# Attention scores from the second batch on as three products of high and low parts, and feed-forward steps of twelve matmuls

## The chip, the core and the metric

One NeuronCore of a Trainium2 chip runs the whole program. The metric is the device time of one execution in microseconds; the kernel before takes 808.25 us (median of 3 runs, 807.92 to 809.6).

## What is computed

For batch 4, 8 heads, sequence 576 and head size 64, in float32:

```
q, k = rotate(q), rotate(k)
p = softmax(q @ k.T / sqrt(64));  x = p @ v            # x: 4 x 576 x 512
xk, xr = mu_k*x + (1-mu_k)*prev(x), mu_r*x + (1-mu_r)*prev(x)
x2 = sigmoid(xr @ w_r) * (relu(xk @ w_k)**2 @ w_v)     # 512 -> 1024 -> 512
h = relu(x2 @ w_in);  u, v = halves of h               # 512 -> 2 x 512
v = normalized rows of v;  v = w_spatial @ v + b
out = (u * v) @ w_out
```

## The kernel before, in words

PE is the TensorE matrix engine, DVE VectorE, ACT ScalarE, POOL GpSimd, SP the engine whose queue issues the DMAs. A matrix product comes in two forms. A product of float32 operands is exact; each is two instructions on PE, and each of these passes its columns twice. In the other form every operand is split into a high part (a copy rounded to fp32r, made by ACT) and a low part (the remainder, a subtraction on DVE), and three single-pass products are summed: high x high, low x high and high x low. The feed-forward and all later layers use the second form, the attention the first.

Heads are worked in pairs: one head of a pair lies in partitions 0 to 63, the other in 64 to 127 (`HEAD`), so that a [128, 576] tile holds q or k of two heads, transposed. There are 16 pairs of heads, `i = 4 * batch + p`. `prep(i)` (L213) loads a "raw" tile of k and one of q (each 128 x 2 x 576), multiplies it by cosines and sines (`times`, L229, DVE) and adds the two halves into a "rot" tile (`rope`, L234, DVE). Three raw and six rot buffers turn; a raw load waits until the sum of the tile three before is done, and a sum waits until the scores of the pair of heads three back are computed.

The attention runs in 72 units (`unit(m)`, L258), nine for two pairs of heads. A plain unit has 128 rows of q of both heads of one pair; every fifth of nine, the tail unit, has the last 64 rows of both pairs at once. A unit's `scores` (L267) are four products: two halves of 288 columns times the two heads. For a plain unit they read 64 partitions each, so the two heads use the upper and the lower row half of PE; the results go to two PSUM tiles of two banks. In a tail unit eight products use 64 x 64 quarters. Then come two maxima on DVE (L280), two exponentials on ACT (L285), transposes of the weights on PE (`turn`, L313 to L324, tile t), their copies by ACT and DVE (`take`, L334), the product with v on PE (`values`, L347, tile v, in column halves) and the final scaling (`gather`, L358, L360). The scores of the next unit wait for both exponentials of this one.

`feed(b, h)` (L399) is the feed-forward of one half (288 rows) of a batch: eight sums over four chunks (tile mk, L443, 12 matmuls each, in two steps of six), their relu, square and split, and four sums over eight chunks (tile mv, L483, 24 matmuls each, in four steps of six), copied by ACT to vs (L489) and stored (L492). The feed-forward of a batch is mixed with the attention of the next batch; that of the last batch comes after the attention. After all attention steps, `close` frees their memory and opens the buffers for the later layers' weights, which are loaded and split then.

No engine's order of work is written out by hand. Each step is added to a `Plan` with an engine, an estimated duration, what it depends on, a rank and, for some, a buffer to take; `Plan.order` (L59) plays the steps through, and takes for each engine, among the steps ready soonest (for engines other than PE within 0.3 us), the one of lowest rank. The instructions are issued in the order that comes out, and each engine keeps to it. Estimated durations only set the order.

The later layers (L602 on) are not touched.

Of the kernel before, what the change touches and what calls it, by code (L numbers as in the profile page):

```python
# [7 lines left out]
F32 = mybir.dt.float32  # L8
# [9 lines left out]
NP = H // 2  # L18
# [6 lines left out]
NFIRST = 2  # L25
WB, GB, WB2, GB2 = 3, 2, 3, 2
RAW, ROT, VB, PFB, PTB, XTS = 3, 6, 3, 3, 2, 6
KB, RLB, VSB = 4, 2, 4
WAIT = 0.3
# [3 lines left out]
def raw(ap):  # L33
    return ap.bitcast(F32)


class Step:


    def __init__(self, eng, us, fn, deps, rank, after, take, give, port):  # L40
        self.eng, self.us, self.fn, self.rank, self.after = eng, us, fn, rank, after
        self.take, self.give, self.slot = take, give, None
        self.port = port or eng == "POOL"
        self.deps = [d for d in deps if d is not None]
        self.end = self.begin = None


class Plan:
# [5 lines left out]
    def add(self, eng, us, fn, deps=(), rank=0.0, after=0.12, take=None, give=None, port=False):  # L54
        s = Step(eng, us, fn, deps, rank, after, take, give, port)
        self.steps.append(s)
        return s

    def order(self):  # L59
# [3 lines left out]
        left, port = len(self.steps), {"DVE": 0.0, "POOL": 0.0}  # L63
        while left:
            best = None
            for e, steps in todo.items():
                ready = []
                for s in steps:
                    if any(d.end is None for d in s.deps) or s.take and not room[s.take]:
                        continue  # L70
                    ready.append((max([free[e]] + [d.end + d.after for d in s.deps]
                                      + ([min(room[s.take])[0]] if s.take else [])
                                      + ([port["POOL" if e == "DVE" else "DVE"]] if s.port else [])), s))
                if ready:
                    soon = min(t for t, _ in ready) + (WAIT if e != "PE" else 0.0)
                    t, s = min((x for x in ready if x[0] <= soon), key=lambda x: (x[1].rank, x[0]))
# [12 lines left out]
            todo[s.eng].remove(s)  # L89
            left -= 1  # L90
# [8 lines left out]
def body(ctx: ExitStack, tc, qp, kp, vp, cs, mu_k, mu_r, w_k, w_v, w_r, w_in, w_sp, b_sp, w_out, out):  # L99
# [19 lines left out]
    cst = at.tile([128, 2, S], F32, name="cst")  # L119
    ident = const.tile([128, 128], F32, name="ident")  # L120
# [76 lines left out]
    def constants():  # L197
# [3 lines left out]
        nc.gpsimd.memset(ident, 0.0)  # L201
        nc.gpsimd.affine_select(out=ident, in_=ident, compare_op=ALU.not_equal, fill=1.0, base=0,
# [10 lines left out]
    def prep(i):  # L213
# [5 lines left out]
        for k in (1, 0):  # L219
# [22 lines left out]
            ropes["n", n] = add("DVE", 0.77, rope, [a] + last, need - 2.5, port=True)  # L242
# [15 lines left out]
    def unit(m):  # L258
# [8 lines left out]
        def scores():  # L267
            ps = st["s"] = [ps_s.tile([128, 2, 512], F32, tag="s", name=f"s{2 * m + j}") for j in range(2)]
            for u, (i, c) in enumerate(w):
# [7 lines left out]
            st["sm"] = at.tile([128, 4, 2], F32, tag="sm", bufs=4, name=f"sm{m}")  # L277
# [90 lines left out]
        scored[m] = s = add("PE", 2.2 if tail else 1.25, scores, need + [exps.get((m - 1, j)) for j in range(2)], m - 1.0)  # L368
# [12 lines left out]
        for n in range(3):  # L381
            turned[m, n] = add("PE", (0.55, 0.55, 0.3)[n], lambda slot, n=n: turn(n, slot), ready[n], m + 0.1 * n, take="t")
# [3 lines left out]
        if tail or part:  # L386
            v = add("PE", 1.6 if tail else 2.5, values, ev + [vloads[i] for i, _ in w], m + 0.9, take="m")
# [11 lines left out]
    def feed(b, h):  # L399
# [35 lines left out]
        for fc in range(NFC):  # L435
            def k_dot(n, slot=None, fc=fc):
# [3 lines left out]
                k = 6 * n  # L440
                for c in (2 * n, 2 * n + 1):
# [22 lines left out]
            z = add("PE", 0.84, lambda slot, k_dot=k_dot: k_dot(0, slot), done + wk_ready + [second.get("close")], rank(fc), take=room)  # L464
            p = add("PE", 0.84, lambda k_dot=k_dot: k_dot(1), [z], rank(fc) - 1)
# [9 lines left out]
        for dc in range(4):  # L475
            def v_dot(n, slot=None, dc=dc):
                if n == 0:
                    xs["v", dc] = bank(slot, f"mv{b}_{h}_{dc}")
                k = 6 * n
                for fc in (2 * n, 2 * n + 1):  # L480
# [13 lines left out]
            z = p = add("PE", 0.84, lambda slot, v_dot=v_dot: v_dot(0, slot), kk + wv_ready, rank(8 + 2 * dc), take=room)  # L494
            for n in range(1, 4):
                p = add("PE", 0.84, lambda n=n, v_dot=v_dot: v_dot(n), [p], rank(8 + 2 * dc) - 1)
# [33 lines left out]
    for m in range(NU):  # L530
# [303 lines left out]
```

## Time and profile before

| | |
|---|---|
| median of three runs | 808.25 us |
| the profiled execution | 808.49 us |
| its span (first to last instruction) | 806.5 us |
| PE, DVE, ACT, POOL busy | 766.6, 497.3, 443.6, 112.0 us |
| granted TensorE clock, mean | 0.991 of 2.4 GHz |

The span is shorter than the time of its execution by 2.0 us. In the profile, L275 is line 275 of the kernel. PE is the stream of matmuls, PEld that of its weight loads, which run beside it; an instruction's duration on PE holds its way through the pipeline, so successive instructions overlap and the distance between their starts tells what each takes of PE. A row's "x8" merges eight like instructions in succession: the first number is the start of the first, the second the time from there to the end of the last. "s" is the tile of the scores, "mk" and "mv" are the feed-forward's sums, "t" transposes, "v" the product with v. SPq is the DMA queue of SP.

### The profile page before, as it was taken

Reading aid. Unit: us, or ns where it says so; the run is one execution under the profiler, and the core shown is the slowest. Engines: PE = TensorE matmul, PEld = TensorE weight load, DVE = VectorE, ACT = ScalarE, POOL = GpSimd, SP = SyncE. Lnnn points to the kernel's source line nnn. Section 1 sums busy time; section 2 is a strip of 40 time slices with the busy share of each in tenths; the row PEclk is TensorE's granted clock in tenths of the full one; section 3 lists DMA queues with packets and bytes.
Section 4 is the critical chain, followed back from the end, with each engine's and each line's share of the span. In section 5 each row is a group of like instructions: output and inputs, shape, how many; then the busy total and the mean of one; then the engine's idle time right before and its main releaser. Section 6 shows DMA issues by size and latency. Waiting matters only on the chain.

```text
span 806.5 us, 14201 instructions
## 1 busy us (share of the span) xinstructions
PE 766.6 (95%) x5736; PEld 654.4 (81%) x5736; DVE 497.3 (62%) x885; ACT 443.6 (55%) x988; POOL 112.0 (14%) x128
## 2 busy tenths in 40 slices
PE   3898889999999999999999999988999999999998
PEld 2465557887887887887887899887999999998997
DVE  4988888966656746646635539889855242635211
ACT  3778786766756756756746755546533422523311
POOL 1332325000000000000000005564410000201000
PEclk9989999999999999999999999999999999999999
DMA  9445440431131131120110033375210202010101
GB/s 323 143 142 174 130 150 30 128 113 60 46 106 60 45 108 59 43 80 1 39 38 2 23 116 113 119 238 189 77 40 26 93 16 89 31 30 1 59 1 60
DMA packets 27555, 67.34 MB, mean 84 GB/s; under 512 B 4001, under 2 KB 8097, under 8 KB 27490
## 3 DMA queue, kind: packets, MB, share of 16 engines
q1 hardware_dynamic: 27490, 66.44, 25.2%
q8 instruction: 45, 0.74, 0.4%
q14 instruction: 20, 0.16, 0.1%
HBM read 52.26 MB, written 14.16 MB: 82 GB/s over the span
## 4 chain that ended last, share of the span: by engine, by line
PE 78%; DVE 8%; ACT 6%; issue 3%; DMA 3%; POOL 2%; SPq 0%; DVEq 0%; POOLq 0%; ACTq 0%
PE s L275 11%; PE v L347 11%; PE mv L483 10%; PE mk L443 9%; PE t L321 8%; PE sp L617 7%; PE o L617 6%; PE hv L681 5%; PE u L617 5%; PE r L617 4%; ACT pf L285 2%; PE t L313 1%; DMA I-120_121<-w_k 1%; DVE rl L453 1%; PE t L324 1%
## 5 line engine op out<-in xcount | busy, mean ns | idle before, releaser
L280 DVE TENSOR_REDUCE sm<-s 128x1 f32<-128x576 f32 x144 | 105.9, 751 | 37.0 <-PE s L275 36.2
L483 PE MATMUL mv<-kh,wv 128*128 128x288 f32 x512 | 117.0, 305 | 1.5 <-ACT kh L457 1.5
L443 PE MATMUL mk<-x,wk 128*128 128x288 f32 x768 | 117.4, 302 | 0.0
L285 ACT ACTIVATE pf<-s,sm 128x576 f32<-128x576 f32 x144 | 106.8, 744 | 15.8 <-DVE sm L280 14.3
L275 PE MATMUL s<-rot,rot 64*128 64x288 f32 (+1 forms) x640 | 103.6, 439 | 11.1 <-DVE rot L234 11.1
L334 ACT COPY pt<-t 128x512 f32<-128x512 f32 x144 | 83.2, 585 | 48.7 <-PE t L321 44.9
L443 PEld LDWEIGHTS mk<-x,wk 128*128 128x128 f32 x768 | 103.9, 188 | 6.1 <-issue 3.1
L321 PE MATMUL t<-ident,pf 128*128 128x128 f32 x512 | 81.7, 283 | 15.6 <-ACT pf L285 15.6
L483 PEld LDWEIGHTS mv<-kh,wv 128*128 128x128 f32 x512 | 85.8, 189 | 11.0 <-issue 9.2
L321 PEld LDWEIGHTS t<-ident,pf 128*128 128x128 f32 x512 | 57.8, 141 | 43.6 <-issue 19.0
L347 PE MATMUL v<-pt,vt 128*64 128x256 f32 (+1 forms) x960 | 92.2, 336 | 0.0
L275 PEld LDWEIGHTS s<-rot,rot 64*128 64x128 f32 (+1 forms) x640 | 57.5, 182 | 35.0 <-issue 11.1
L347 PEld LDWEIGHTS v<-pt,vt 128*64 128x64 f32 x960 | 56.2, 141 | 27.5 <-issue 7.2
L483 PE MATMUL mv<-kl,wv 128*128 128x288 f32 x256 | 75.7, 296 | 0.5 <-DVE kl L461 0.4
L617 PE MATMUL r<-xr,wr 128*128 128x288 f32 x384 | 53.4, 297 | 3.0 <-ACT vs L489 1.0
L617 PE MATMUL u<-x,wi 128*128 128x288 f32 x384 | 53.6, 302 | 2.5 <-ACT us L715 2.5
L617 PEld LDWEIGHTS u<-x,wi 128*128 128x128 f32 x384 | 53.0, 194 | 3.0 <-ACT us L715 2.8
L617 PEld LDWEIGHTS r<-xr,wr 128*128 128x128 f32 x384 | 51.6, 188 | 4.4 <-ACT rr L640 1.5
L229 DVE TENSOR_TENSOR raw<-raw,cst 128x1152 f32<-128x1152 f32 x32 | 44.5, 1389 | 16.9 <-DMA raw<-kp 9.2
L617 PE MATMUL sp<-ws,vn 128*128 128x288 f32 x384 | 53.9, 295 | 0.0
L617 PE MATMUL o<-g,wo 128*128 128x288 f32 x384 | 52.9, 296 | 0.5 <-ACT os L737 0.5
L617 PEld LDWEIGHTS sp<-ws,vn 128*128 128x128 f32 x384 | 52.4, 188 | 0.7
(332 smaller groups left out, 1091.5 us busy)
## 6 DMA issues: line engine op xcount, KB each, us to landing
raw<-kp SPq DMA_DIRECT2D x15, 576.0 KB, 4.9
raw<-qp SPq DMA_DIRECT2D x15, 576.0 KB, 3.8
vt<-vp SPq DMA_DIRECT2D x16, 320.0 KB, 3.7
xd<-xt SPq DMA_DIRECT2D x16, 288.5 KB, 3.1
vd<-vs SPq DMA_DIRECT2D x32, 144.0 KB, 1.8
v<-vd SPq DMA_DIRECT2D x16, 288.0 KB, 2.8
out<-os SPq DMA_DIRECT2D x16, 288.0 KB, 2.1
x<-xd SPq DMA_DIRECT2D x12, 288.5 KB, 3.0
```

What stands on the lines that cost most here:

```text
L229: nc.vector.tensor_tensor(t["raw", k], t["raw", k], cst, op=ALU.mult)
L275: nc.tensor.matmul(o, q[r, 128 * c:min(128 * c + 128, S)], k[r, h * HALF:(h + 1) * HALF], start=True, stop=True)
L280: nc.vector.tensor_reduce(st["sm"][:, 0, j:j + 1], st["s"][j][:, :, :HALF], axis=AX.XY, op=ALU.max, negate=True)
L285: nc.scalar.activation(st["p"][:, j, :].rearrange("p (a b) -> p a b", a=2), st["s"][j][:, :, :HALF], AF.Exp, bias=st["sm"][:, 0, j:j + 1], ...
L313: nc.tensor.transpose(pt.rearrange("p c (h q) -> p (c h) q", h=2)[:, 4 * u + c, :], p[HEAD[n], u, k:k + 128], ident[HEAD[n], HEAD[n]])
L321: nc.tensor.transpose(pt[:, c, :], p[:, n, k:k + 128], ident)
L334: nc.scalar.copy(o, x) if eng == "ACT" else nc.vector.tensor_copy(o, x)
L347: nc.tensor.matmul(o, v[:, 4 * j + c if c < 4 else 8 + j, :], a, start=c == 0, stop=c == 4)
L443: nc.tensor.matmul(ps[:, :HALF], wk[w][:, c, fc * 128:(fc + 1) * 128], a[:, c, :], start=k == 0, stop=k == 11)
L483: nc.tensor.matmul(xs["v", dc][:, :HALF], wv[w][:, fc, dc * 128:(dc + 1) * 128], a, start=k == 0, stop=k == 23)
L617: nc.tensor.matmul(ps[:, h, :HALF], w, a[:, h * HALF:(h + 1) * HALF], start=m == 0, stop=m == n - 1)
L681: nc.tensor.matmul(ps[:, :FS], x[a][:, d, c:c + 128], wi[w][:, d, FS:], start=k == 0, stop=k == 11)
```

## The change

From the second batch on (`EXACT = NP`, pairs of heads 4 to 15), q and k are split after the sum into a high part (ACT) and a low part (DVE), and the scores are three single-pass products in place of one exact product. In a plain unit these are still in row halves, twelve instructions in place of eight. In a tail unit, the 64 tail rows of both heads are also copied (high) and subtracted (low) into the two diagonal blocks of a 128 x 128 tile whose other blocks are zero (`ends`), so that the tail's products use the whole array: twelve instructions in place of sixteen. The sum is written over the raw tile, which so stays in use until the low part is there. Raw buffers go from 3 to 2; the six rot buffers become four for exact sums and high parts together, and four more for low parts; the buffers for vs go from 4 to 2. The scores of the pair of heads two back, not three back, now hold up the high copy. The feed-forward's steps have twelve matmuls in place of six, the same products in the same order. The planner's estimates for PE are new (with 0.1 us added when the kind of step changes), for existing steps too.

```diff
+EXACT = NP
-RAW, ROT, VB, PFB, PTB, XTS = 3, 6, 3, 3, 2, 6
-KB, RLB, VSB = 4, 2, 4
-WAIT = 0.3
+RAW, ROT, VB, PFB, PTB, XTS = 2, 4, 3, 3, 2, 6
+KB, RLB, VSB = 4, 2, 2
+WAIT, SWITCH, BONUS = 0.3, 0.1, 0.0
...
             s.begin, s.end = t, t + s.us
+            if s.eng == "PE" and s.kind != kind:
+                kind = s.kind
+                s.end += SWITCH
...
+    ends = [[at.tile([128, 128], F32R, tag=f"qe{i}{k}", name=f"qe{i}{k}") for k in range(2)] for i in range(2)]
...
             def rope(k=k):
-                x = t.pop(("raw", k))
-                y = t[k] = at.tile([128, S], F32, tag="rot", bufs=ROT, name=f"rot{i}_{k}")
+                x = t["raw", k]
+                y = t[k] = x[:, 0, :] if i >= EXACT else at.tile([128, S], F32, tag="rh", bufs=ROT, name=f"rot{i}_{k}")
                 nc.vector.tensor_tensor(y, x[:, 0, :], x[:, 1, :], op=ALU.add)
+            def high(k=k):
+                t["hi", k] = at.tile([128, S], F32R, tag="rh", bufs=ROT, name=f"rh{i}_{k}")
+                nc.scalar.copy(t["hi", k], t[k])
+                if k == 0:
+                    for j in range(2):
+                        nc.scalar.copy(ends[i % 2][0][HEAD[j], 64 * j:64 * j + 64], t[k][HEAD[j], 512:])
+            def low(k=k):
+                t["lo", k] = at.tile([128, S], F32R, tag="rl", bufs=ROT, name=f"rl{i}_{k}")
+                nc.vector.tensor_tensor(t["lo", k], t[k], raw(t["hi", k]), op=ALU.subtract)
+                if k == 0:
+                    for j in range(2):
+                        r, z = HEAD[j], slice(64 * j, 64 * j + 64)
+                        nc.vector.tensor_tensor(ends[i % 2][1][r, z], t[k][r, 512:], raw(ends[i % 2][0][r, z]),
+                                                op=ALU.subtract)
...
-            ropes["n", n] = add("DVE", 0.77, rope, [a] + last, need - 2.5, port=True)
+            if i < EXACT:
+                ropes["n", n] = add("DVE", 0.77, rope, [a] + last, need - 2.5, port=True)
+            else:
+                a = add("DVE", 0.77, rope, [a], need - 2.5, port=True)
+                a = add("ACT", 0.67 if k else 1.1, high, [a] + last, need - 2.5)
+                ropes["n", n] = add("DVE", 0.76 if k else 1.2, low, [a], need - 2.5, port=True)
...
+            if w[0][0] >= EXACT:
+                for u, (i, c) in enumerate(w):
+                    t = qk[i]
+                    for n, (a, b) in enumerate((("hi", "hi"), ("hi", "lo"), ("lo", "hi"))):
+                        for h in range(2):
+                            x, f = slice(h * HALF, h * HALF + HALF), dict(start=n == 0, stop=n == 2)
+                            if tail:
+                                nc.tensor.matmul(ps[u][:, h, :HALF], ends[i % 2][a == "lo"], t[b, 1][:, x], **f)
+                            else:
+                                for j, r in enumerate(HEAD):
+                                    nc.tensor.matmul(ps[j][:, h, :HALF], t[a, 0][r, 128 * c:128 * c + 128], t[b, 1][r, x], **f)
+                return
...
-        scored[m] = s = add("PE", 2.2 if tail else 1.25, scores, need + [exps.get((m - 1, j)) for j in range(2)], m - 1.0)
+        scored[m] = s = add("PE", (2.0 if tail else 1.07) if w[0][0] < EXACT else 1.58 if tail else 0.8, scores, need + [exps.get((m - 1, j)) for j in range(2)], m - 1.0, kind="s")
...
-            z = add("PE", 0.84, lambda slot, k_dot=k_dot: k_dot(0, slot), done + wk_ready + [second.get("close")], rank(fc), take=room)
-            p = add("PE", 0.84, lambda k_dot=k_dot: k_dot(1), [z], rank(fc) - 1)
+            z = p = add("PE", 1.58, lambda slot, k_dot=k_dot: k_dot(0, slot), done + wk_ready + [second.get("close")], rank(fc), take=room)
...
-            for n in range(1, 4):
-                p = add("PE", 0.84, lambda n=n, v_dot=v_dot: v_dot(n), [p], rank(8 + 2 * dc) - 1)
+            for n in range(1, 2):
+                p = add("PE", 1.58, lambda n=n, v_dot=v_dot: v_dot(n), [p], rank(8 + 2 * dc) - 1)
...
-            if i not in ropes and i >= ROT // 2 and max(which_last(i - 3)) <= m:
+            if i not in ropes and i >= ROT // 2 and max(which_last(i - ROT // 2)) <= m:
```

## Rows read from the trace of the kernel before

**Rows 1.** The page: busy us (share of the span) by engine; the chain by engine.

```profile
PE 766.6 (95%) x5736; PEld 654.4 (81%) x5736; DVE 497.3 (62%) x885; ACT 443.6 (55%) x988; POOL 112.0 (14%) x128
...
PE 78%; DVE 8%; ACT 6%; issue 3%; DMA 3%; POOL 2%; SPq 0%; DVEq 0%; POOLq 0%; ACTq 0%
```

**Rows 2.** Windows: length, busy PE, PEld, DVE, ACT, POOL (count), clock, DMA, GB/s.

```profile
60.00:117.00 57.00, 49.00 (x366) 31.90 (x364) 49.94 (x97) 45.65 (x111) 15.42 (x14) 0.97 0.47 151
117.00:180.00 63.00, 62.60 (x510) 51.11 (x509) 53.46 (x91) 41.85 (x104) 12.28 (x15) 1.00 0.30 95
180.00:240.00 60.00, 59.94 (x486) 48.36 (x486) 37.55 (x72) 37.92 (x95) 0.20 (x2) 1.00 0.22 71
```

**Rows 3.** PE's waits, 0 to 117 us, then 117 to 470 (total, times, longest).

```profile
PE t L321 <- ACT pf L285: 15.2, 11, 2.3
PE s L275 <- DVE rot L234: 11.1, 1, 11.1
...
PE t L321 <- ACT pf L285: 0.4, 1, 0.4
```

**Rows 4.** Timelines of two short windows, PE: pairs of one score block.

```profile
408.11 0.65 PE L275 MATMUL s<-rot,rot 64*128 64x288 f32 x3
...
408.35 0.64 PE L275 MATMUL s<-rot,rot 64*128 64x288 f32 x3
```

**Rows 5.** Timeline, PE: the score block of a plain unit and its neighbours.

```profile
414.84 0.29 PE L483 MATMUL mv<-kh,wv 128*128 128x288 f32 x1
415.06 1.24 PE L275 MATMUL s<-rot,rot 64*128 64x288 f32 x8
416.24 0.40 PE L483 MATMUL mv<-kh,wv 128*128 128x288 f32 x1
416.47 0.29 PE L483 MATMUL mv<-kl,wv 128*128 128x288 f32 x1
```

**Rows 6.** The same timeline: a long feed-forward run and a tail unit.

```profile
428.17 3.43 PE L443 MATMUL mk<-x,wk 128*128 128x288 f32 x24
431.44 0.60 PE L321 MATMUL t<-ident,pf 128*128 128x128 f32 x4
431.96 2.16 PE L275 MATMUL s<-rot,rot 64*64 64x288 f32 x16
434.05 0.66 PE L321 MATMUL t<-ident,pf 128*128 128x128 f32 x4
```

**Rows 7.** Timelines of short windows, weight loads (PEld).

```profile
400.77 0.19 PEld L483 LDWEIGHTS mv<-kh,wv 128*128 128x128 f32 x1
400.88 0.19 PEld L483 LDWEIGHTS mv<-kl,wv 128*128 128x128 f32 x1
...
407.76 0.30 PEld L275 LDWEIGHTS s<-rot,rot 64*128 64x128 f32 x4 [0.17 <-issue]
```

**Rows 8.** Groups by form, DVE, then ACT: busy us, mean ns | idle before, releaser.

```profile
L229 DVE TENSOR_TENSOR raw<-raw,cst 128x1152 f32<-128x1152 f32 x32 | 44.5, 1389 | 16.9 <-DMA raw<-kp 9.2 <-DMA raw<-qp 7.6
...
L461 DVE TENSOR_TENSOR kl<-rl,kh 128x576 fp32r<-128x576 f32 x32 | 24.3, 760 | 5.4 <-ACT kh L457 5.1
...
L304 DVE COPY pe<-pf 128x64 f32<-128x64 f32 x32 | 5.9, 227 | 0.6
...
L457 ACT CAST kh<-rl 128x576 fp32r<-128x576 f32 x32 | 21.5, 673 | 8.5 <-DVE rl L453 7.9
```

**Rows 9.** The chain that ended last, in order of time: an earlier tail unit.

```profile
129.32 2.09 PE s L275 x16
```

**Rows 10.** The page: groups of DVE and ACT in the chain of a unit.

```profile
L280 DVE TENSOR_REDUCE sm<-s 128x1 f32<-128x576 f32 x144 | 105.9, 751 | 37.0 <-PE s L275 36.2
```

**Rows 11.** The page: DMA issues, KB each, us to landing.

```profile
raw<-kp SPq DMA_DIRECT2D x15, 576.0 KB, 4.9
...
vd<-vs SPq DMA_DIRECT2D x32, 144.0 KB, 1.8
```

**Rows 12.** The DMA queue's own waits (total, times, longest).

```profile
SPq L224 <- DVE rot L234: 110.2, 19, 19.9
```

More of the change, by code (lines that the diff above doesn't have):

```diff
@@ L37, with __init__ @@
 class Step:
-    def __init__(self, eng, us, fn, deps, rank, after, take, give, port):
+    def __init__(self, eng, us, fn, deps, rank, after, take, give, port, kind):
         self.eng, self.us, self.fn, self.rank, self.after = eng, us, fn, rank, after
         self.take, self.give, self.slot = take, give, None
-        self.port = port or eng == "POOL"
+        self.port, self.kind = port or eng == "POOL", kind
         self.deps = [d for d in deps if d is not None]
@@ L52, in __init__, with add @@
         self.steps, self.room = [], room
-    def add(self, eng, us, fn, deps=(), rank=0.0, after=0.12, take=None, give=None, port=False):
-        s = Step(eng, us, fn, deps, rank, after, take, give, port)
+    def add(self, eng, us, fn, deps=(), rank=0.0, after=0.12, take=None, give=None, port=False, kind=None):
+        s = Step(eng, us, fn, deps, rank, after, take, give, port, kind)
         self.steps.append(s)
@@ L62, in order @@
         todo = {e: [s for s in self.steps if s.eng == e] for e in free}
-        left, port = len(self.steps), {"DVE": 0.0, "POOL": 0.0}
+        left, port, kind = len(self.steps), {"DVE": 0.0, "POOL": 0.0}, None
         while left:
@@ L75, in order @@
                     soon = min(t for t, _ in ready) + (WAIT if e != "PE" else 0.0)
-                    t, s = min((x for x in ready if x[0] <= soon), key=lambda x: (x[1].rank, x[0]))
+                    t, s = min((x for x in ready if x[0] <= soon), key=lambda x: (x[1].rank - (BONUS if e == "PE" and x[1].kind == kind else 0.0), x[0]))
                     if best is None or t < best[0]:
@@ L201, in constants @@
         nc.gpsimd.memset(ident, 0.0)
+        for x in ends[0] + ends[1]:
+            nc.gpsimd.memset(raw(x), 0.0)
         nc.gpsimd.affine_select(out=ident, in_=ident, compare_op=ALU.not_equal, fill=1.0, base=0,
@@ L268, in scores @@
             ps = st["s"] = [ps_s.tile([128, 2, 512], F32, tag="s", name=f"s{2 * m + j}") for j in range(2)]
+            st["sm"] = at.tile([128, 4, 2], F32, tag="sm", bufs=4, name=f"sm{m}")
+            if w[0][0] >= EXACT:
[10 more added lines that the diff above has]
+                return
             for u, (i, c) in enumerate(w):
@@ L276, in scores @@
                                          start=True, stop=True)
-            st["sm"] = at.tile([128, 4, 2], F32, tag="sm", bufs=4, name=f"sm{m}")
         def top(j):
@@ L381, in unit @@
         for n in range(3):
-            turned[m, n] = add("PE", (0.55, 0.55, 0.3)[n], lambda slot, n=n: turn(n, slot), ready[n], m + 0.1 * n, take="t")
+            turned[m, n] = add("PE", (0.44, 0.44, 0.22)[n], lambda slot, n=n: turn(n, slot), ready[n], m + 0.1 * n, take="t", kind="t")
             eng = ("ACT", "ACT", "DVE")[n]
@@ L386, in unit @@
         if tail or part:
-            v = add("PE", 1.6 if tail else 2.5, values, ev + [vloads[i] for i, _ in w], m + 0.9, take="m")
+            v = add("PE", 1.1 if tail else 2.2, values, ev + [vloads[i] for i, _ in w], m + 0.9, take="m", kind="v")
             for u, (i, c) in enumerate(w):
@@ L439, in k_dot @@
                 ps, (xh, xl) = xs["k", fc], xs["x"]
-                k = 6 * n
-                for c in (2 * n, 2 * n + 1):
+                k = 0
+                for c in range(NP):
                     for a, w in ((xh, 0), (xl, 0), (xh, 1)):
@@ L478, in v_dot @@
                     xs["v", dc] = bank(slot, f"mv{b}_{h}_{dc}")
-                k = 6 * n
-                for fc in (2 * n, 2 * n + 1):
+                k = 12 * n
+                for fc in range(4 * n, 4 * n + 4):
                     kh, kl = (t[:, fc % 2, :] for t in xs["kk", fc // 2])
```

2 lines of the change are left out of this document (1 added, 1 removed).

## The prediction

> **What bounds the kernel now.** I read the page's shares first: PE is busy for 95% of the span and PE lines make 78% of the chain that ended last [rows 1]. A share is an average, so the windows come next. The reader is to see three stages there. Until about 115 us the first batch's attention runs alone: PE is busy for 49.0 of 57 us and DVE for 49.9. From 117 to 470 us the attention of the other three batches is mixed with the feed-forward of the batch before: PE is busy for 59.9 of every 60 us, DVE for 53.5 of 63 at first and some 37.5 of 60 later, ACT for about 38. The granted clock is 0.97 to 1.00, the upper of its two levels, 2.4 GHz [rows 2]. The last 336 us belong to code that the change does not touch, save for the feed-forward of the last batch. A busy PE may be a PE that waits inside its pipeline, so the third view is PE's waits: in the first batch 11.1 us for the first scores and 15.2 for exponentials, and from 117 to 470 no more than 0.4 us in all [rows 3]. In those 353 us nothing but PE's own work sets the pace, so whatever PE is spared there moves the end of the attention, if DVE and ACT can still follow. What is after hangs on that end: `close` waits for all attention steps, and the later layers' weights are loaded behind it.
>
> **Scores of a plain unit (48 units, L275).** Today's eight instructions (four products, each passed through PE as two) come as pairs, one per row half; successive pairs start 0.24 us apart (408.11, 408.35) [rows 4]. Four pairs are 0.97 us. The block takes more than that: from the feed-forward product before it (414.84) it starts 0.22 us later where such products follow each other in 0.13; from its start to the next product are 1.18; and that product takes 0.23 where 0.13 is usual [rows 5]. In all 0.09 + 1.18 + 0.10 = 1.37 us, so 0.40 are for getting into the row halves and out. I take those 0.40 over unchanged: the new block is in row halves too.
>
> The new block has six pairs of single-pass products of 288 columns. The trace has no such pair. Its nearest row is the feed-forward product of the same type and width on the full array, 0.13 us apart (0.132 each over the 24 from 428.17 to 431.44, less 0.10 for the first) [rows 6]. That the two halves run beside each other is what the pairs show: an exact instruction streams its columns twice, which by the transposes (128 columns in (431.96 - 431.44 - 0.09)/4 = 0.108) is 0.24 for 288 columns, and a pair takes just that [rows 4, 6]. So a pair is 0.132, six are 0.79, and a plain unit gives back 0.97 - 0.79 = 0.18: **48 x 0.18 = 8.6 us**. Bounds: 0.12 a pair (half of 0.243) gives 11.7; products one after another, 12 x 0.132 = 1.58, cost 29 (rival below).
>
> Weights are loaded twelve times, not eight. The four loads of the first two pairs are done in 0.30 us where one takes 0.19, so the second pair is 0.11 behind the first; single loads of the full array also start 0.11 apart (400.77, 400.88) [rows 7]. Two half loads take the time of one full load, 0.11, and hide below 0.132. The Trainium skill (TensorE: Matmul & The Clock Gate, LDWEIGHTS) says that loading takes time by columns and no less with fewer rows, which speaks against this change; if the twelve loads queued one by one, its 107 ns would make about 1.28 us of a block, and the sum would turn into a loss of some 11 us. The rows differ for two loads of different halves, and I go by the rows.
>
> **Scores of a tail unit (6 units).** Today: 0.09 to enter and 2.09 from 431.96 to 434.05, 2.18 in all [rows 6]. New: twelve full-array products, 12 x 0.132 = 1.58, which stand beside transposes and feed-forward on the full array and so have no row halves or quarters to get into. What the step still costs is at most the 0.10 seen behind a score block [rows 5], and I set it off against the like cost behind today's block, which I left out. The zero blocks are written once at the start. **6 x 0.60 = 3.6 us** (bounds 3 and 4.2).
>
> **Feed-forward in steps of twelve.** The products are the same. From the last product of a run to the transpose behind it there is no gap beyond 0.13 (the 24 products of [rows 6]), and the 0.40 of a score block is paid once a unit whatever its neighbours, so merging saves little: **0.5 us**, at most one entry of 0.05, half of 0.10, for each of 54 units, 2.7. What it may cost is attention that becomes ready just after a step of 1.58 us has begun; that is PE time used, not lost, while the chain s, two maxima, one exponential (1.2 + 1.5 + 0.9, some 3.6 us, the maximum 0.75 [rows 10]) is far below the 6.7 us of a unit ((431.96 - 129.32)/45, tail to tail [rows 6, 9]). I take nothing, and make the other case a rival.
>
> **High and low parts of q and k (12 pairs of heads).** DVE gets per pair two subtractions of 0.76 and two small ones of 0.23; ACT two copies of 0.67 and two small ones, which I put at half of that at most [rows 8]. That is 2.0 us each a pair, 24 in all. Cover: from 180 us DVE has 37.6 + 8 = 45.5 of 57.6 us per batch and ACT the same, 79%, below the 85% at which DVE stood from 117 to 180 without PE waiting [rows 2]. In 117 to 180, three pairs add 6 to DVE's 53.5, and one pair of heads fewer is prepared ahead (bufs 6 to 4), which takes 2 x 1.39 for the products with cosines and sines and 2 x 0.76 for the sums away, 4.3 [rows 8]: about 55 of 60, 91%. The first batch stood at 88% and PE waited there. I put **2 us** of new waits there, between 0 and 9 (15.2 us of waits over 18 units [rows 3], for the eleven units of that window).
>
> **First batch.** Its scores stay exact. Pair 4 and perhaps 5 are split there: 2 us of DVE each, on an engine at 88%. Raw buffers go from 3 to 2, so the second pair of heads' first load now waits for the first sum, which is done just before the first scores at 11.1 [rows 3]; it lands 4.9 us later [rows 11], and its scores are those of the fifth unit. Loads behind it on SP's queue are placed by the planner. **1.5 us** slower, between -1 and 4.
>
> **Queues.** Raw loads already hold SP's queue for 110 us in 19 waits [rows 12], with stores of vs and xt and loads of v behind them. From the second batch a raw buffer stays until the low part exists: 4.9 to land, 1.4 for the product, 0.8 for the sum, 0.7 and 0.8 for the two parts, and the wait for the scores two pairs back. A pair of heads has about 30 us, so both buffers turn in time. A vs store lands in 1.8 us [rows 11] and the same buffer is wanted two outputs, 6.3 us, later: two instead of four cost nothing; if late, ACT waits, and then the bank.
>
> **Sum.** The profiled execution took 808.5 us (806.5 of span and 2.0 around it), as good as the median of 808.25. -8.6 - 3.6 - 0.5 + 2 + 1.5 = -9.2: **799.3 us**.
>
> **Rivals.**
> A. *As summed*: 791 to 804 (0.12 a pair and no new waits; or waits of 7 us).
> B. *DVE or ACT takes PE's place* until about 180 us: 4 us in the first batch and 9 after, against 13 gained: 808.5, no change. For it: 91% and 88%. Against: DVE waited for others there for some 10 of 63 us, and steps are ordered by the planner, which counts the new work. 804 to 813.
> C. *The halves do not run side by side for single-pass products*, in each of the 48 plain score blocks. It decides above (0.97 + 0.08)/6 = 0.175 us a pair (0.08 is a 48th of the 3.6 of the tails). Products in line, 0.264 a pair, give 48 x 0.61 = 29, and 808.5 + 29 - 4.1 + 3.5 = 837. Loads in line, 2 x 0.11 a pair, give 48 x 0.35 = 17 and 825. Against: both loads and products of two halves start together in the exact form. Slower.
> D. *Long feed-forward steps make attention late*: half of the added 0.79 us on each of 54 units, 21 us, if the chain of a unit set the pace: about 820. Against: 3.6 of 6.7 us. A part of it, 812, is likelier.
> E. *Not doing what it says*: the switch at EXACT = NP is plain in the code; no chance of its own.
>
> **Numbers.** A 0.70, B 0.15 (0.05 faster, 0.06 same, 0.04 slower), C 0.07, D 0.08 (0.01 same). About 0.2%, 1.6 us, can be told from no change. Faster 0.75, same 0.07, slower 0.18. The range 791 to 812 leaves out C, most of D and the edges of A and B, some 0.18; A's own range is 791 to 804.
>
> **What would show it.** Score pairs 0.12 to 0.14 us apart and blocks of about 1.0 us to the next product; tails of 1.6; units 6.5 us apart from 117 us on; PE waits below 3 us in that stretch; `close` 8 to 12 us earlier, and the stages after it as long as before. PE waits on `low` or on exponentials would speak for B or D, score blocks above 1.3 us for C. I am wrong if PE is no longer without waits there.

## The result, and the profile after

The changed kernel takes 795.91 us (median of four executions, 793.3 to 797.58) against 808.09. The ratio on record is 0.9836, with a 95% interval of 0.9811 to 0.986 (the two medians alone would give 0.985); the percentages below go by such ratios. The forecast was 799.3 us in a range of 791 to 812, with rival A the likeliest. The profiled execution took 797.47 us, with a span of 795.4.

The page of the kernel after, the lines that answer to [rows 1]:

```profile
PE 752.4 (95%) x5904; PEld 664.2 (84%) x5904; DVE 509.7 (64%) x933; ACT 461.2 (58%) x1036; POOL 112.9 (14%) x132
...
PE 83%; DVE 5%; ACT 4%; DMA 3%; issue 3%; POOL 1%; SPq 0%; ACTq 0%; DVEq 0%; POOLq 0%
```

PE has 168 instructions more and 14.2 us less to do; DVE has 12.4 us more and ACT 17.6. The windows of the kernel after, with the columns of [rows 2], and the stretch in the middle by itself:

```profile
60.00:117.00 57.00, 50.81 (x408) 34.21 (x404) 50.96 (x104) 48.71 (x121) 15.09 (x14) 1.00 0.44 137
117.00:180.00 63.00, 60.16 (x501) 52.10 (x499) 52.50 (x94) 43.61 (x107) 13.91 (x15) 0.92 0.28 89
180.00:240.00 60.00, 60.00 (x540) 52.33 (x540) 43.54 (x85) 43.01 (x108) 0.20 (x2) 1.00 0.24 72
142.40:152.70 10.30, 9.24 (x42) 7.32 (x44) 8.28 (x12) 6.03 (x16) 3.42 (x2) 0.50 0.01 2
```

From 180 us to the end of the attention PE is still never idle, and DVE and ACT stand at 73% and 72% there: they have room for the new parts. Between 117 and 180 the granted clock is now 0.92. PE's waits in the kernel after, first from 0 to 117 us and then from 117 to 470, which answer to [rows 3]:

```profile
PE t L361 <- ACT pf L325: 11.9, 10, 1.8
PE s L316 <- DVE rot L241: 10.6, 1, 10.6
...
PE t L361 <- ACT pf L325: 2.2, 1, 2.2
PE t L364 <- ACT rb L336: 0.7, 1, 0.7
```

Two new waits, 2.9 us in all, stand where 0.4 were. Now the score blocks, against [rows 4 to 6] (timeline of PE after, a plain unit at 165 us, then a tail unit and what follows it):

```profile
164.49 0.60 PE L361 MATMUL t<-ident,pf 128*128 128x128 f32 x4
165.02 0.53 PE L308 MATMUL s<-rh,rh 64*128 64x288 f32 x4
165.38 0.43 PE L308 MATMUL s<-rl,rh 64*128 64x288 f32 x4
165.65 0.42 PE L308 MATMUL s<-rh,rl 64*128 64x288 f32 x4
166.00 0.66 PE L361 MATMUL t<-ident,pf 128*128 128x128 f32 x4
...
304.79 0.42 PE L305 MATMUL s<-rh,qe 128*128 128x288 f32 x2
...
306.39 0.60 PE L361 MATMUL t<-ident,pf 128*128 128x128 f32 x4
...
306.93 0.27 PE L364 MATMUL t<-ident,rb 128*128 128x128 f32 x1
306.96 1.83 PE L483 MATMUL mk<-x,wk 128*128 128x288 f32 x12
308.72 2.38 PE L387 MATMUL v<-pt,vt 128*64 128x256 f32 x20
311.03 0.54 PE L308 MATMUL s<-rh,rh 64*128 64x288 f32 x4
...
312.04 1.86 PE L483 MATMUL mk<-x,wk 128*128 128x288 f32 x12
313.82 1.02 PE L353 MATMUL t<-ident,pf 64*128 64x64 f32 x16
```

and the weight loads (PEld) at the start of the same plain block:

```profile
165.02 0.30 PEld L308 LDWEIGHTS s<-rh,rh 64*128 64x128 f32 x4 [0.17 <-issue]
```

Four products of the two halves take 0.27 us (165.38 to 165.65): two pairs, 0.135 each. The plain block takes 0.98 from its start to the next transposes, where the exact one took 1.18, and the tail 1.60 (304.79 to 306.39) where it took 2.09. One more thing is to be seen: twelve feed-forward products take 1.76 us (306.96 to 308.72) and 1.78 (312.04 to 313.82), 0.18 to 0.20 more than 12 x 0.132. It is tempting to call that the price of a visit to the feed-forward, but most of it is there without the visit too. The transpose ahead of the first visit takes 0.03 (306.93 to 306.96) where 0.108 is usual, and four transposes followed by scores at once take 0.53 (164.49 to 165.02), 0.10 more than 4 x 0.108. So from the last transpose to the product with v (306.93 to 308.72) 1.79 pass, 0.21 more than the twelve products; with no visit the last of the four transposes takes 0.53 - 3 x 0.108 = 0.21 as well (the three times in units 36 to 63 that a product with v follows transposes at once, it is 0.20). A visit costs something where it stands right behind a score block or a product with v: from 311.03 to 313.82 less 1.58 are 1.21, where a block followed by transposes of 128 rows takes 0.98.

To see where the time went, the span is cut at the starts of units 18, 27 and 71. Worked out from the first score product of each unit on PE's timeline, in us:

```
                    to unit 18   18 to 27   27 to 71   from 71   span
before                 104.4       60.6      294.0      347.5    806.5
after                  101.0       64.0      281.6      348.8    795.4
```

The 44 units from 27 on give 12.4 us, 0.28 each; the nine before them cost 3.4; the stages after the attention are about as long as before (+1.3). The 3.4 of the first batch can't be put down to the change alone: in the kernel before, the granted clock stood at its lower level for 10.2 us there, after not at all (1.00 in its window against 0.97 in [rows 2]).

### The profile page after: what moved, and what is told of

Read it like the earlier page. It is cut to its first block, busy times and chain, and to the rows that moved or that the text cites. A ratio compares the mean times of both kernels' runs of the same rounds, so it can differ in the third digit from the quotient of the medians.

```text
span 795.4 us, 14650 instructions
## 1 busy us (share of the span) xinstructions
PE 752.4 (95%) x5904; PEld 664.2 (84%) x5904; DVE 509.7 (64%) x933; ACT 461.2 (58%) x1036; POOL 112.9 (14%) x132
## 4 chain that ended last, share of the span: by engine, by line
PE 83%; DVE 5%; ACT 4%; DMA 3%; issue 3%; POOL 1%; SPq 0%; ACTq 0%; DVEq 0%; POOLq 0%
PE mk L483 11%; PE v L387 11%; PE mv L522 10%; PE t L361 9%; PE sp L656 7%; PE o L656 6%; PE s L308 6%; PE u L656 6%; PE r L656 5%; PE hv L720 5%; PE s L316 3%; ACT pf L325 1%; PE s L305 1%; ACT pt L374 1%; PE t L364 1%
## 5 line engine op out<-in xcount | busy, mean ns | idle before, releaser
L483 PE MATMUL mk<-x,wk 128*128 128x288 f32 x768 | 114.3, 301 | 0.0
L522 PE MATMUL mv<-kh,wv 128*128 128x288 f32 x512 | 112.1, 303 | 0.0
L361 PE MATMUL t<-ident,pf 128*128 128x128 f32 x512 | 83.4, 286 | 14.1 <-ACT pf L325 14.1
L361 PEld LDWEIGHTS t<-ident,pf 128*128 128x128 f32 x512 | 57.6, 142 | 37.4 <-issue 15.4
L656 PE MATMUL r<-xr,wr 128*128 128x288 f32 x384 | 56.6, 308 | 5.3 <-ACT xr L616 2.7
L656 PEld LDWEIGHTS r<-xr,wr 128*128 128x128 f32 x384 | 54.7, 199 | 6.8 <-ACT xr L616 3.2
L656 PEld LDWEIGHTS o<-g,wo 128*128 128x128 f32 x384 | 51.7, 188 | 1.4 <-ACT os L776 1.2
L522 PEld LDWEIGHTS mv<-kl,wv 128*128 128x128 f32 x256 | 48.8, 191 | 0.6 <-DVE kl L501 0.6
```

The lines of the kernel that those rows point to most:

```text
L361: nc.tensor.transpose(pt[:, c, :], p[:, n, k:k + 128], ident)
L483: nc.tensor.matmul(ps[:, :HALF], wk[w][:, c, fc * 128:(fc + 1) * 128], a[:, c, :], start=k == 0, stop=k == 11)
L522: nc.tensor.matmul(xs["v", dc][:, :HALF], wv[w][:, fc, dc * 128:(dc + 1) * 128], a, start=k == 0, stop=k == 23)
L656: nc.tensor.matmul(ps[:, h, :HALF], w, a[:, h * HALF:(h + 1) * HALF], start=m == 0, stop=m == n - 1)
```

## The experiments

All twelve start from the kernel after. Theory "scores": the gain is PE time of the score blocks, as summed. Its rivals: the feed-forward's steps give it, or the planner's new estimates do.

**Each of the two parts alone, and neither.** Feed-forward steps of six again, the products and their order as before the change:

```diff
-                k = 0
-                for c in range(NP):
+                k = 6 * n
+                for c in (2 * n, 2 * n + 1):
...
-            z = p = add("PE", 1.58, lambda slot, k_dot=k_dot: k_dot(0, slot), done + wk_ready + [second.get("close")], rank(fc), take=room)
+            z = add("PE", 0.79, lambda slot, k_dot=k_dot: k_dot(0, slot), done + wk_ready + [second.get("close")], rank(fc), take=room)
+            p = add("PE", 0.79, lambda k_dot=k_dot: k_dot(1), [z], rank(fc) - 1)
...
-                for fc in range(4 * n, 4 * n + 4):
+                for fc in (2 * n, 2 * n + 1):
```

> The changed kernel with the feed-forward again in steps of six matmuls (estimate 0.79 us each), all else as changed. Theory: the gain is the shorter scores, and the steps' length matters little: 796 to 798 us, at most 2 more than the changed kernel; the score block costs the same 1.06 us of PE a unit, and t and mk cost some 0.1 us a unit more because single steps come more often between s, v and t. Rival (the merged steps are a main part of the gain, as a unit went from 6.68 to 6.40 us where the scores alone explain 0.22): 800 us or more.

Exact scores everywhere, with the steps of twelve, the new estimates and the buffers of the change:

```diff
-EXACT = NP
+EXACT = B * NP
```

> The changed kernel with exact scores in every batch (the switch set past the last pair of heads), its buffer counts, planner estimates and feed-forward steps of twelve kept. Theory: all of the gain but 1 to 3 us is gone, 804 to 808 us, since the PE time per unit from 165 us on goes back by 0.22 x 44 = 10 us and only the order of steps stays better. Rival (order, estimates and merged steps make the gain, and the split's extra work on DVE and ACT eats what the scores give): 798 us or less.

And both edits together, which leaves of the change only its estimates and its buffers:

> The changed kernel with exact scores in every batch and feed-forward steps of six: the fourth corner beside the changed kernel, steps of six with split scores, and steps of twelve with exact scores. What is left of the change are fewer buffers, new planner estimates and the 0.1 us for a change of kind. Theory (the shorter scores and the longer steps act each by itself, the estimates do nothing): 806 to 810 us, a ratio to the kernel before of 0.997 to 1.002, and a unit in the stretch of units 36 to 63 takes 6.72 to 6.78 us. Rival (the estimates set a better order by themselves): 802 to 804 us, 6.60 to 6.65 us a unit.

Measured, as ratios to the kernel before, with their intervals:

```
                  steps of six               steps of twelve
exact scores      1.0017 (1.0001 to 1.0033)  0.9934 (0.991 to 0.9959)
split scores      0.9956 (0.9935 to 0.9977)  0.9836 (0.9811 to 0.986)
```

The estimates and buffers alone gain nothing. The split scores give 0.98% (8 us) with steps of twelve and 0.61% (5 us) with six; the steps of twelve give 0.83% (6.7 us) with exact scores and 1.20% (9.7 us) with split ones. So both parts pay, each clear of noise, and the steps far more than was expected of them. That each pays more beside the other (by 0.37%) is not clear of the four intervals taken together; the unit times below speak for it, from one execution of each kernel. Units 36 to 63 show how; in all but one of these kernels PE does the same instructions there save for the scores (from the starts on PE's timeline, us per unit; f is mk and mv; a visit is a run of feed-forward between two other kinds):

```
                      all     s      t      f      v     visits
before               6.745  1.282  1.175  3.116  1.172   2.11
exact, six           6.660  1.277  1.054  3.156  1.173   2.30   (6 of 576 products of f fewer)
exact, twelve        6.609  1.273  1.114  3.050  1.173   1.56
split, six           6.534  1.065  1.130  3.166  1.173   2.19
split, twelve        6.379  1.061  1.108  3.038  1.173   1.56
```

From exact to split the unit gets 0.230 us shorter with steps of twelve, of which s is 0.212. From six to twelve it gets 0.155 shorter with split scores. The column f falls by 0.128 with just the same products, but it holds waits too, and what a visit takes from the transposes ahead of it. In the kernel with steps of six and split scores, PE's waits from 117 to 470 us, then those in units 36 to 63 (225.4 to 401.9 us):

```profile
PE t L361 <- ACT pf L325: 8.0, 6, 2.1
PE s L308 <- ACT pf L325: 1.1, 2, 0.9
...
PE t L361 <- ACT pf L325: 2.4, 3, 1.8
```

and a piece of its PE timeline:

```profile
326.87 0.29 PE L523 MATMUL mv<-kh,wv 128*128 128x288 f32 x1
327.49 0.66 PE L361 MATMUL t<-ident,pf 128*128 128x128 f32 x4 [0.33 <-ACT pf L325]
327.90 0.38 PE L523 MATMUL mv<-kh,wv 128*128 128x288 f32 x1
328.12 0.29 PE L523 MATMUL mv<-kl,wv 128*128 128x288 f32 x1
...
328.87 0.53 PE L308 MATMUL s<-rh,rh 64*128 64x288 f32 x4
...
329.85 0.40 PE L523 MATMUL mv<-kh,wv 128*128 128x288 f32 x1
```

The wait at 327.49 falls into f: that product has 0.62 to itself (326.87 to 327.49), not 0.13. The 2.4 us of waits are 0.09 a unit, and with steps of twelve there are none in these units. The rest, some 0.05 a unit, is an estimate from the starts on PE's timeline: 16 of the 59 visits in these 27 units stand right behind a score block or a product with v, where a visit adds some 0.1 to 0.3 us beyond its products, and 6 of 42 with steps of twelve. From 117 to 470 us the waits are 9.1 us here, 4.1 with exact scores and steps of six, 1.6 with exact scores and twelve, 2.9 after. So more than half of what the steps of twelve give beside split scores is waits: 9.1 - 2.9 = 6.2 of 9.7 us. That faster scores make exponentials the later event, and that a longer step behind each visit covers it, fits these numbers but was not tested by itself: the steps of six were run with one set of the planner's estimates, and by the estimates alone the waits change as much (below).

**Longer steps still.** The product with w_v as one step of 24:

```diff
-                k = 12 * n
-                for fc in range(4 * n, 4 * n + 4):
+                k = 0
+                for fc in range(NFC):
...
-            z = p = add("PE", 1.58, lambda slot, v_dot=v_dot: v_dot(0, slot), kk + wv_ready, rank(8 + 2 * dc), take=room)
-            for n in range(1, 2):
-                p = add("PE", 1.58, lambda n=n, v_dot=v_dot: v_dot(n), [p], rank(8 + 2 * dc) - 1)
+            z = p = add("PE", 3.16, lambda slot, v_dot=v_dot: v_dot(0, slot), kk + wv_ready, rank(8 + 2 * dc), take=room)
```

> The changed kernel with each of the feed-forward's four output sums (24 matmuls) as one step in place of two of twelve. Theory (each visit to the feed-forward costs some 0.1 us of PE, so longer steps help as long as attention has its slack): visits to the feed-forward fall by some 0.2 a unit, 0.02 us a unit, 1 us; but one step of 3.2 us is most of the slack of a unit's chain (3.6 of 6.4 us), so PE waits of 0 to 6 us: ratio 0.981 to 0.990. Rival (PE is saturated whatever the steps, and the gain of doubling repeats): ratio below 0.979.

Measured 0.9891 (0.9873 to 0.9909), 800.65 us: slower than after. Visits fall further, to 1.22 a unit, and f to 2.980, but t rises from 1.108 to 1.221, so that a unit takes 6.436 us for 6.379. PE waits 5.1 us from 117 to 470, 1.2 of them in units 36 to 63, where after has none, and 13.7 us ran at the lower clock level before unit 71, where after had 10.2. Fewer visits give no more here, and attention is late: rival D of the prediction, at a step twice as long. How much of the loss is waits and how much clock was not taken apart.

**The halves in line.** The same twelve products of a plain unit, six of the upper row half first and then six of the lower (in a tail unit nothing changes):

```diff
-                    for n, (a, b) in enumerate((("hi", "hi"), ("hi", "lo"), ("lo", "hi"))):
-                        for h in range(2):
...
-                                for j, r in enumerate(HEAD):
+                    for j, r in enumerate((HEAD[0],) if tail else HEAD):
+                        for n, (a, b) in enumerate((("hi", "hi"), ("hi", "lo"), ("lo", "hi"))):
+                            for h in range(2):
```

> The changed kernel with the twelve products of a plain unit ordered by head: six of the upper row half, then six of the lower; the same products and loads, nothing left out. Theory (the gain needs the two halves side by side): neighbours in one half follow each other 0.12 to 0.13 us apart, a block is about 0.66 us longer (five of the six pairs of a half in line), 48 units give some 30 us: 820 to 832 us. Rival (a half product is cheap for another reason, and the order does not matter): within 3 us of the changed kernel.

Measured 817.21 us in one execution, beside 809.43 of the kernel before. A unit's s is 1.390 us, 0.33 more than after. A block on its PE timeline:

```profile
352.16 0.53 PE L308 MATMUL s<-rh,rh 64*128 64x288 f32 x2
352.53 0.29 PE L308 MATMUL s<-rl,rh 64*128 64x288 f32 x1
352.54 0.40 PE L308 MATMUL s<-rh,rh 64*128 64x288 f32 x1
352.67 0.30 PE L308 MATMUL s<-rl,rh 64*128 64x288 f32 x1
352.77 0.29 PE L308 MATMUL s<-rh,rh 64*128 64x288 f32 x1
352.80 0.29 PE L308 MATMUL s<-rh,rl 64*128 64x288 f32 x1
...
353.17 0.42 PE L308 MATMUL s<-rh,rl 64*128 64x288 f32 x2
353.52 0.66 PE L361 MATMUL t<-ident,pf 128*128 128x128 f32 x4
```

The block takes 1.36 to the transposes, not 0.98. Within a half, products start 0.13 apart (352.54 is the lower half's first, 352.53 and 352.67 the upper half's third and fourth). So two products take the time of one only when they lie in different halves, which is what rival C denied; and the loss is smaller than six further products (0.79), because the lower half's products begin while the upper half still has three to come.

**The split in the first batch too.**

```diff
-EXACT = NP
+EXACT = 0
```

> The changed kernel with the split scores in the first batch too. Theory (in the first batch PE is not alone in setting the pace, it waits there 14 us for exponentials behind a DVE and ACT at 85 to 90%): 4 pairs of heads add 8 us to DVE and ACT, 16 plain and 2 tail units spare PE 0.22 x 16 + 0.6 x 2 = 4.7 us; 797 to 803 us, slower than the changed kernel by 1 to 6. Rival (PE sets the pace there too): 790 to 794 us.

Measured 1.0073 (1.0048 to 1.0098), 815.94 us: 20 us worse than after, where 1 to 6 were expected. PE's waits in its first 200 us:

```profile
PE t L361 <- ACT pf L325: 15.2, 10, 2.4
PE s L308 <- ACT rh L245: 12.3, 1, 12.3
PE s L308 <- ACT pf L325: 4.9, 4, 2.3
```

and its window from 60 to 117 us:

```profile
60.00:117.00 57.00, 46.77 (x342) 35.40 (x341) 44.96 (x88) 40.08 (x99) 11.85 (x11) 0.79 0.33 111
```

The first 18 units take 11 us more than after, the next nine 10 more. PE does less (46.8 of 57 us against 50.8) and is granted 0.79 of its clock; DVE and ACT do less too (45.0 and 40.1 us against 51.0 and 48.7), so neither is at its limit over that window. Without the wait for the first scores, PE waits 24 us in the first 172, where after waits 18, and 51 us run at the lower clock level before unit 71, where after had 10.2. The 6 us of waits are too few for the loss; the lower level, at which a score block takes 2.10 us for 0.98 (below), is large enough for it. The runs do not tell the two apart, nor show that DVE and ACT by themselves set the pace. What they show is that the split, worth 8 us from the second batch on, costs 20 in the first, where PE waits for exponentials already.

**Two more pairs exact, and low parts on POOL.** Both aim at the 3.4 us lost between units 18 and 27.

```diff
-EXACT = NP
+EXACT = NP + 2
```

> The changed kernel with the split from pair of heads 6 on in place of 4, so nine units (18 to 26) keep exact scores and pairs 4 and 5 cost no high and low parts. Theory (in those units DVE's extra work costs more than the shorter scores give): 9 x 0.22 = 2 us are lost and the wait with its half clock, about 6 us, is avoided: units 18 to 27 take 59 to 61 us, 791 to 794 us, ratio 0.978 to 0.982. Rival (the wait there is a matter of the order and comes anyway): 797 to 800 us.

```diff
-                nc.vector.tensor_tensor(t["lo", k], t[k], raw(t["hi", k]), op=ALU.subtract)
+                nc.gpsimd.tensor_tensor(t["lo", k], t[k], raw(t["hi", k]), op=ALU.subtract)
...
-                ropes["n", n] = add("DVE", 0.76 if k else 1.2, low, [a], need - 2.5, port=True)
+                ropes["n", n] = add("POOL", 1.6 if k else 2.4, low, [a], need - 2.5)
```

> The changed kernel with the low parts of q and k made by POOL in place of DVE (the same subtractions, estimates 1.6 and 2.4 us). Theory (PE's wait of 2.2 us at 140 us, and the half clock of 10 us right behind it, come from DVE, which the split has brought to its limit while the weights of w_v are still being made): the wait goes or shrinks, units 18 to 27 take 58 to 61 us in place of 64, 790 to 794 us, ratio 0.977 to 0.981. Rival (POOL, which is busy with the same weights, is late instead, or slows DVE by sharing its port): 797 us or more, ratio above 0.986.

The first (0.9829, 0.9807 to 0.985) can't be told from after: units 18 to 27 take 62.0 instead of 64.0, with exact scores among them, and the first 18 units of its profiled execution 3.5 us more. The second is slower (0.9907, 0.9888 to 0.9926): units 18 to 27 take 65.1, 10.2 us still run at the lower clock level, and 27 to 71 take 283.0 for 281.6. In the group of the low parts one takes POOL nearly twice DVE's 750 ns (min, median and max in ns):

```profile
L252 POOL TENSOR_TENSOR rl<-raw,rh x24: 1409/1425/2215, 79.8 to 400.4; 128x576 fp32r<-128x576 f32 x24
```

PE's waits from 117 to 165 us come to 3.8, not the 2.9 of after. So taking the low parts off DVE does not take the waits away; a late POOL may have put others in their place. The view of the wait in the kernel after says what is ahead of the late exponential (timelines of PE, DVE and ACT around it):

```profile
140.34 0.27 PE L364 MATMUL t<-ident,rb 128*128 128x128 f32 x1
142.80 1.11 PE L361 MATMUL t<-ident,pf 128*128 128x128 f32 x4 [2.18 <-ACT pf L325]
...
138.92 1.24 DVE L160 TENSOR_SCALAR I-1426_1427<-I-1426_1427 128x512 int32<-128x512 int32 x1
140.19 0.69 DVE L161 SCALAR_TENSOR_TENSOR I-1613_1614<-I-1613_1614,I-1426_1427 128x512 int32<-128x512 int32 x1
...
141.13 0.75 DVE L320 TENSOR_REDUCE sm<-s 128x1 f32<-128x576 f32 x1
...
141.91 0.74 ACT L325 ACTIVATE pf<-s,sm 128x576 f32<-128x576 f32 x1 [0.89 <-DVE sm L320]
```

DVE works on the split of the feed-forward's weights (L160, L161) from 138.92 on and takes the maximum only at 141.13; the exponential and PE's transposes wait in turn. From 142.4 us on, before that wait is over, the granted clock stands at 0.50 in the windows above, 1.2 GHz, for 10.3 us. The next score block on PE:

```profile
143.84 1.21 PE L308 MATMUL s<-rh,rh 64*128 64x288 f32 x4
...
145.94 0.47 PE L361 MATMUL t<-ident,pf 128*128 128x128 f32 x1
```

It takes 2.10 us to the transposes, where 0.98 is usual.

**What the planner's price does.** The 0.1 us for a change of kind taken out, then taken out but added to the estimates of the steps (0.1 to s and v, 0.08 to the two longer steps of t and to each of f), then doubled:

```diff
-WAIT, SWITCH, BONUS = 0.3, 0.1, 0.0
+WAIT, SWITCH, BONUS = 0.3, 0.0, 0.0
```

> The changed kernel with the planner's 0.1 us for a change of kind on PE set to 0; only the order of steps can differ. Theory (steps of twelve alone bring the fewer changes between row halves, column halves and full array): within 1.5 us of the changed kernel, ratio 0.982 to 0.986, 6.36 to 6.42 us a unit from 36 to 63. Rival (the planner puts v right before s because a change is priced): 6.45 us a unit or more, 3 to 6 us slower than the changed kernel, ratio 0.987 to 0.992.

> The changed kernel with no price for a change of kind, but with the same time (some 0.45 us a unit) put into the estimates of PE's steps themselves: s and v 0.10 more, transposes 0.08, feed-forward steps 0.08. Theory (what the price does is to bring the planned PE time of a unit up to the real one; without it the plan lets PE run ahead of ACT and DVE, and PE waits): within 3 us of the changed kernel, ratio 0.980 to 0.987, PE's waits from 117 to 470 us below 4 us. Rival (the price must stand at a change of kind, since that is where the order is chosen): ratio 0.992 or more, as with the price at 0.

> The changed kernel with 0.2 us for a change of kind in place of 0.1, about 0.5 us a unit more in the plan than PE takes. Theory (the order is best where the planned PE time is near the real one): PE waits for exponentials more often, ratio 0.986 to 0.992, slower than the changed kernel by 2 to 6 us. Rival (more price, fewer changes, better): 6.30 us a unit or less from unit 36 to 63, ratio below 0.981.

Without the price: 1.0051 (1.0032 to 1.007), 813.86 us, which loses the whole gain. PE changes kind less often than after (4.70 times a unit against 4.96, units 36 to 63), so the price does not work by keeping changes down. PE's waits of that kernel from 117 to 470 us, and a window:

```profile
PE t L361 <- ACT pf L325: 7.8, 4, 3.1
...
117.00:165.00 48.00, 43.22 (x346) 35.61 (x346) 40.56 (x71) 32.34 (x77) 15.09 (x11) 0.86 0.21 66
```

They come to 10.1 us in all, and 23.9 us before unit 71 run at the lower clock level. With the same time put into the steps, 0.9857 (0.9834 to 0.9881), nearly all is back; doubled, 0.982 (0.9799 to 0.9841), which can't be told from after, though a loss was expected. So it is the planned time that counts, not where it stands, and only one side of it was seen to cost: with PE's steps planned too short, PE waits on the chip, mostly for exponentials; planned longer by as much again, nothing is lost.

Last, a bonus for staying with the same kind:

```diff
-WAIT, SWITCH, BONUS = 0.3, 0.1, 0.0
+WAIT, SWITCH, BONUS = 0.3, 0.1, 0.5
```

> The changed kernel with BONUS = 0.5, by which the planner prefers a ready step of the kind just done unless another is half a unit more urgent. Theory (fewer changes between the forms of PE save PE time in the saturated stretch): 6.28 to 6.34 us a unit from unit 36 to 63, 2 to 5 us faster than the changed kernel, ratio 0.977 to 0.981. Rival (attention is put off and its exponentials come late): PE waits above 5 us from 117 to 470 us, ratio 0.985 or more.

Measured 0.9993 (0.9972 to 1.0014), 809.57 us. PE's waits for exponentials in the first 117 us are 18.1 us (11.9 after), and the first 18 units take some 12 us longer; 17 us there run at the lower clock level, where after has none. From 117 to 470 PE waits 6.2 us, and units 36 to 63 take 6.44 us each, where less than the 6.38 of after was expected: the rival's case. That a preference by kind passes over the steps that feed the slower engines is the likely reason, not shown by itself.

No version here is faster than after by more than the intervals; doubling the price and two more exact pairs together were not tried.

## Why the prediction was right, and where it was not

The time, the likeliest case and the bound were right; one term of the sum, the feed-forward's, was wrong by a factor of over ten.

- **What bounds it**: right. From 117 us on PE's time is the time, save for 2.9 us of waits and one stretch at the lower clock level, and the later stages did not change.
- **Scores**: right. 8.6 + 3.6 = 12.2 us were forecast; 0.230 us a unit from exact to split, over 54 units, are 12.4, and s alone, 0.212, makes 11.4. Less the 2 and 1.5 us put down for waits and the first batch, the split was to give 8.7; the runs give 8 with steps of twelve, and 5 with six. The two halves' products run beside each other (0.135 us a pair, 0.132 forecast), the cost of getting into the halves and out stayed, and the tail takes 1.60 (1.58 forecast).
- **Loads**: right. Twelve loads hide in a block of 0.98 us: four into the two halves are done in 0.30 (165.02), the time of two full loads 0.11 apart [rows 7]. By the Trainium skill (TensorE: Matmul & The Clock Gate, LDWEIGHTS) a load takes time by its columns and no less with fewer rows; twelve of 128 columns, one after the other, are by its formula 1.28 us, an estimate. The trace agrees for one load (0.18 us for 64 rows, 0.19 for 128), but has no such queue: loads into different halves run beside each other. (The 11 us of loss given for that case leave out the 3.5 us of the other terms; with them it is 14.)
- **Feed-forward in steps of twelve: the step that failed.** The text put "0.5 us, at most one entry of 0.05, half of 0.10, for each of 54 units, 2.7"; measured were 6.7 us with exact scores and 9.7 with split ones. The price of a visit was not far off: a visit between transposes is free, as the text says [rows 6], and the fewer visits behind score blocks and products with v give some 0.05 us a unit. What failed is "PE time used, not lost", "I take nothing": the sum had no waits of PE that the length of the steps could change, and saw in long steps only a risk. With faster scores and steps of six PE has 9.1 us of waits, with steps of twelve 2.9. Another 1.8 us lie behind the start of unit 71 (350.6 us with steps of six, 348.8 with twelve), where the last batch's feed-forward runs; what it is there stays open.
- **New waits, 2 us (0 to 9)**: 2.9 us from 117 to 470, at the place named, just below the 3 us that the text set as a sign. What was not foreseen is the stretch at half the clock: 9.2 us of PE work at 0.50, some 4.6 more than at the upper level by the score block of 2.10 us. Units 18 to 27 take 3.4 us more than before even so with faster scores in them.
- **High and low parts**: the new steps take 23.2 us of DVE and 21.9 of ACT (24 each forecast); in all DVE has 12.4 and ACT 17.6 more. From 180 us on they are covered. The forecast of 79% put the 8 us of four pairs of heads into 57.6 us, where by the text's own 30 us a pair only two fall; with 4 us it is 72%, and 73% and 72% were measured.
- **First batch, +1.5 us**: open. The profiled executions differ by -3.4, with another clock in the two.
- **Sum**: -9.2 forecast, -12.2 by the medians and -13.3 by the ratio. By the runs' ratios that is +1.4 for the estimates and buffers, which the sum left out, -6.7 for the feed-forward's steps, then -8 for the scores with their parts and waits. That the time came out only 3.4 us from the forecast is in part luck: of the 6 us or more that the sum missed in the steps, the estimates and the stretch at the lower clock level, which it missed too, took some back.

Rivals: **A** holds. **B** shows at most in units 18 to 27, where PE's wait follows DVE's work; whether it is what costs 20 us with the first batch split is open, since the clock fell there too. **C** is refuted by the pairs and by the run in line. **D** fits the loss at steps of 24; at twelve the opposite is true, PE waits less than with six. That the planner's estimates alone make the gain is refuted by the exact scores with steps of six (1.0017).

## What to carry to other kernels

Price a change of kind against the row in which it is absent: of the 0.18 us that a visit shows, 0.08 is missing from the transposes ahead, and 0.10 is paid without the visit too. And before calling a regrouping of the same products free, ask what it does to the waits that another part of the change will make: here that was more than half of its gain. Split parts stage by stage: the same split gave 8 us where PE hardly waited, and cost 20 where it waited for exponentials already. And an order made by a planner is only as good as its durations: 0.1 us too little a change made 17 us.

## What the runs showed of the hardware that was not expected

- A wait of 2.2 us of PE (140.6 to 142.8) was followed by 10.3 us at a granted clock of 0.50. The sum of the waits does not tell how much of it comes: from 117 to 470 us, 10.1 us of waits went with 17 us at the lower level where the price was taken out, but 9.1 with 6.8 in the run with steps of six and split scores. What in a wait brings the clock down was not taken apart.
- Matmuls of one row half start ahead of matmuls of the other half that come earlier in the program: 352.54 before 352.67 in the run in line.
- The same twelve products on the same halves take 0.98 or 1.36 us by their order alone.
